# Linear attention with squared-ReLU feed-forward, FP32, one core: the first strip attended by pairs of heads, its queries loaded by POOL

## The chip, the cores and the metric

The kernel runs on one core of a Trainium2 chip. A core has five engines with an instruction queue each: PE (TensorE, matrix products and transposes), DVE (VectorE), ACT (ScalarE), POOL (GpSimd) and SP (SyncE, which here only issues DMAs). Each queue runs in order; the engines meet through semaphores. All DMAs, from whatever queue, run on the core's 16 DMA engines. The metric is the time of one execution on the device in microseconds; less is better.

## The reference

Everything is FP32, except that the two weight matrices arrive as 64-bit floats.

```
q, k, v: (8 batches, 8 heads, 576 tokens, 64);  g_norm: (64)
kv  = einsum('bhsd,bhse->bhde', k, v)               # 64 x 64 for each head
o   = einsum('bhsd,bhde->bhse', q, kv)
o   = o / sqrt(mean(o*o, last axis) + 1e-6) * g_norm
x   = o.transpose(0, 2, 1, 3).reshape(4608, 512)
h   = x @ w_in                                      # w_in: (512, 2048)
out = maximum(h, 0)**2 @ w_out                      # w_out: (2048, 512)
```

There is no softmax: queries meet a 64 x 64 state for each head. The key-value product of a head must be finished, over all tokens, before any of its queries can use it.

## The kernel before

**Tiling.** A token tile has 128 tokens (n), a strip has NT = 4 tiles, and there are 9 strips (s). A batch b has C = 4 whole tiles and a rest of 64 tokens; the rests of two batches form one tile. Heads go by pairs p, NP = 4 for a batch, so that a pair fills 128 partitions. Strip 0 is the four whole tiles of batch 0.

**Attention, in steps.** `transposed_query(b, p)` transposes a pair's queries on PE (L312) and copies them out on ACT (L314). `key_value(b, p)` forms k'v of the pair (L330), with the 64 rest tokens as its last two products, and copies the two blocks into a block diagonal on ACT (L332, L333). `query(n)` multiplies a tile's queries by the block diagonals of all four pairs (L362), squares on ACT (L371), sums on DVE (L372), and finds 1/sqrt with a root on ACT and a Newton step on DVE (`inverse_rms`), then scales (L388). `features(n)` transposes the result on PE (L414) and writes it with g_norm into xT (L415), the form that the feed-forward reads. For strip 0 `first_queries` does this for the four tiles together, after all four pairs: all products, then squares and sums tile by tile, one small 1/sqrt chain over 128x32, then scaling and transposes tile by tile.

**Feed-forward.** Strip 0 multiplies with w_in directly (`up_first`: 16 steps of four products, 128x512, L553). Then `down` multiplies with w_out by a scheme of seven products for a 2x2 block product (Strassen-Winograd), named 1 to 7, in two halves i each. Later strips use seven products on both sides. The order is ORDER = (1, 2, 6, 5, 7, 3, 4). Products share PSUM banks by BANK: 1, 6, 7 and 4 in A (of which there are two), 5 and 3 in B, 2 in C. Products 1, 5 and 2 open a bank; the others add into it. `combine` takes what is needed out between them: after 1, 6 and 5 ACT copies the bank into a snapshot (L529), after 2, 7 and 3 DVE adds bank and snapshot into the output.

**Weights.** The weights come as 64-bit floats in 32 pieces (`load_piece`, 512 KB each, eight buffers `raw`): 16 of w_in, 16 of w_out. A piece takes two operations on ACT (`convert_on_act`: L189, L192) and four on DVE (`convert_pieces`: L204, L207, L213, L218). The four buffers `w_c` between them bound how far ACT runs ahead. Pieces are converted two at a time; ACT is two pieces ahead of DVE. `up_first` of group g needs pieces 4g to 4g + 3. For w_out, `sums_out` also forms four sums and stores them; from these stores and those of L662 the blocks w_blk are streamed back (L597). `sums_in` forms the sums of w_in that later strips need, in the places of the first three w_out blocks.

**Order.** Nothing reorders the program: every engine runs its instructions as the Python code emits them. The attention steps stand in the list `slices`, in the order b, p; `attend(n)` emits the list up to n. Before strip 0 the steps of batch 0 are emitted with conversions between them as EARLY says, two conversions (pieces 0 to 3) in all, and ACT's operations for pieces 4 and 5. Then the steps of batch 1 are spread over the strip's up and down steps.

**Queues.** k and v go by SP, so do the pieces. The queries of pairs 0 to 2 of batch 0 go by ACT's queue, that of pair 3 by POOL's, later ones by SP. The rests of batch 0 (k_rest, v_rest, L129) go by ACT. The buffers of q, k and v are three deep: the fourth pair's loads wait until the first pair is used up.

Of the kernel before, what the change touches and what calls it, by code (L numbers as in the profile page):

```python
# [10 lines left out]
I32 = mybir.dt.int32  # L11
# [8 lines left out]
def kernel(  # L20
# [44 lines left out]
    STRIP = NT * P  # L65
    TH = STRIP // 2
    N_STRIP = N_TILE // NT
    EARLY = (0, 0, 0, 1, 1, 1, 1, 2)
    SQ = 32
    Q_ON_PE = 2  # L70
    X_ON_PE = 2
# [21 lines left out]

    def load(b, p, q_eng):
        hs = slice(2 * p, 2 * p + 2)
        for n, src, eng in (("k", k, nc.sync), ("v", v, nc.sync), ("q", q, q_eng)):
            whole = src[b, hs, 0 : C * P].rearrange("h (sp c) d -> sp h c d", c=C)
            if n == "q" and b >= Q_ON_PE:

                t = qkv_pool.tile([P, 4 * C, SQ], FP32, name=n, tag=n)  # L100
                for a in range(4):
                    h, f = divmod(a * SQ, D)
                    eng.dma_start(
                        out=t[ts(a, SQ)],
                        in_=src[b, 2 * p + h, 0 : C * P, f : f + SQ].rearrange("(i k) f -> i k f", k=4 * C),
                    )
            elif n != "q":
                t = qkv_pool.tile([P, 2, C, D], FP32, name=n, tag=n)
                eng.dma_start(out=t, in_=whole)
            else:  # L110

                t = qkv_pool.tile([P, C, 2, D], FP32, name=n, tag=n)
                for h in range(2):
                    eng.dma_start(out=t[:, :, h, :], in_=whole[:, h])
            main[n, b, p] = t
# [9 lines left out]
    def load_rest(b, eng):  # L125
        h = b % 2
        half = slice(REST * h, REST * (h + 1))
        for t, src in ((k_rest[half], k), (v_rest[half, h], v)):
            eng.dma_start(out=t, in_=src[b, :, C * P : S].rearrange("h s d -> s h d"))  # L129
# [20 lines left out]
    def load_next(q_eng=nc.sync):  # L150
        u = next(to_load, None)
        if u is not None:
            load(*u, q_eng)
# [20 lines left out]
    def load_piece():  # L174
        if len(raw) < len(sources):
            t = raw_pool.tile([P, 2, WN // 2], I64, name="raw", tag="raw")
            nc.sync.dma_start(out=t, in_=sources[len(raw)])
            raw.append(t)
# [6 lines left out]
    def convert_on_act(i):  # L185
# [6 lines left out]
        nc.scalar.activation(r, low, AF.Copy, scale=2.0**-29)  # L192
        words[i] = c, r, high

    def convert_pieces(ids, dests):

        for i in range(acted[0], min(ids[-1] + 3, len(sources))):
            convert_on_act(i)
            acted[0] = i + 1
        now = [words.pop(i) for i in ids]  # L200


        for c, _, _ in now:
            nc.vector.tensor_scalar(out=c, in0=c, scalar1=LEAST, scalar2=MOST, op0=ALU.max, op1=ALU.min)  # L204

        for c, _, _ in now:
            nc.vector.tensor_scalar(  # L207
                out=c.bitcast(I32), in0=c.bitcast(I32), scalar1=3, scalar2=0x3FFFFFFF,
                op0=ALU.logical_shift_left, op1=ALU.bitwise_and,
            )  # L210

        for c, _, high in now:
            nc.vector.scalar_tensor_tensor(  # L213
                out=c.bitcast(I32), in0=high, scalar=-(2**30), in1=c.bitcast(I32),
                op0=ALU.bitwise_and, op1=ALU.bitwise_or,
            )
        for (c, r, _), dest in zip(now, dests):
            nc.vector.tensor_tensor(out=dest.bitcast(I32), in0=c.bitcast(I32), in1=r, op=ALU.add)  # L218

        end = ids[-1] + 1  # L220
        while len(raw) < min(end + 8, max(len(sources) - 4, end + 4), len(sources)):
            load_piece()

# [32 lines left out]

    conversions = [(pieces_in, i) for i in range(0, NG * NP, 2)]
    conversions += [(pieces_out, j) for j in range(0, FQ, 2)] + [(sums_out, j) for j in range(0, FQ, 2)]
    converted = [0]

    def convert(n):
        while converted[0] < min(n, len(conversions)):
# [12 lines left out]
    one = const.tile([P, 1], FP32, name="one")  # L275
    nc.vector.memset(one, 1.0)
    nc.scalar.sqrt(one, one)
    load_next(nc.scalar)
    load_rest(0, nc.scalar)
    load_piece()  # L280
    load_piece()
    load_next(nc.scalar)
    load_next(nc.scalar)
    g_col = const.tile([P, 1], FP32, name="g_col")
    g_src = g_norm.rearrange("(d u) -> d u", u=1)
    for h in range(2):
# [36 lines left out]
    def key_value(b, p):  # L323
        tk, tv = main.pop(("k", b, p)), main.pop(("v", b, p))

        ps = apsum.tile([P, D], FP32, name="kv_ps", tag="at")
        for c in range(C + 1):
            for h in range(2):
                a, w = (tk[:, h, c, :], tv[:, h, c, :]) if c < C else (k_rest[:, 2 * p + h], v_rest[:, b % 2, 2 * p + h])
                nc.tensor.matmul(ps[ts(h, D)], lhsT=a, rhs=w, start=c == 0, stop=c == C)  # L330
        d = kv_all[:, (NP * b + p) % (2 * NP + 1)]
        nc.scalar.copy(d[0:D, 0:D], ps[0:D])  # L332
        nc.scalar.copy(d[D:P, D:P], ps[D:P])  # L333
        kvd[b, p] = d
        if b < 2:
            if p == 0:
                load_next(nc.sync if b else nc.gpsimd)
                if b == 0:
                    for _ in range(6):
                        load_piece()  # L340
        else:
            load_next()
            if p == NP - 1 and b + 1 < B:
                load_rest(b + 1, nc.sync)
                load_q_rest(b + 1, nc.sync)
# [16 lines left out]
                nc.tensor.matmul(o, lhsT=qT[b, p][:, c_b, :], rhs=kvd[b, p], start=True, stop=True)  # L362
        return ps

    def inverse_rms(tiles):

        n = len(tiles) * H
        ms = small.tile([P, NT * H], FP32, name="ms", tag="ms")[:, :n]
        for i, ps in enumerate(tiles):
            sq = xn_pool.tile([P, d_model], FP32, name="sq", tag="sq", bufs=1)  # L370
            nc.scalar.activation(sq, ps, AF.Square)  # L371
            nc.vector.reduce_sum(out=ms[:, ts(i, H)], in_=by_head(sq), axis=AX.X)  # L372
        nc.vector.tensor_scalar(out=ms, in0=ms, scalar1=1.0 / D, scalar2=EPS, op0=ALU.mult, op1=ALU.add)
        r = small.tile([P, NT * H], FP32, name="rms", tag="rms")[:, :n]
        nc.scalar.activation(r, ms, AF.Sqrt)
        nc.vector.reciprocal(r, r)

        t = small.tile([P, NT * H], FP32, name="newton", tag="newton")[:, :n]
        nc.vector.scalar_tensor_tensor(out=t, in0=ms, scalar=-0.5, in1=r, op0=ALU.mult, op1=ALU.mult)
        nc.vector.tensor_tensor(out=t, in0=t, in1=r, op=ALU.mult)  # L380
        nc.vector.scalar_tensor_tensor(out=r, in0=t, scalar=1.5, in1=r, op0=ALU.add, op1=ALU.mult)
        return r
# [8 lines left out]

    def query(n):
        ps = products_x(n)
        normalized(n, ps, inverse_rms([ps]))

    def first_queries():

        tiles = [products_x(n) for n in range(NT)]
        r = inverse_rms(tiles)
        for n, ps in enumerate(tiles):  # L400
            normalized(n, ps, r[:, ts(n, H)])
            features(n)

    def open_xt(s):
        if s not in xt:
# [50 lines left out]
    slices, ready = [], {}  # L456
    for b in range(B):
        for p in range(NP):
            slices += [(transposed_query, (b, p)), (key_value, (b, p))]
        first = b // 2 * PAIR + (C if b % 2 else 0)  # L460
        ns = list(range(first, first + C + b % 2))
        if b == 0:
            slices.append((first_queries, ()))
            ready[0] = len(slices)
            continue

        for i in range(len(ns) + 2):
            if i < len(ns):
                slices.append((query, (ns[i],)))
            if 0 < i <= len(ns):  # L470
                slices.append((features if b < X_ON_PE else squares_x, (ns[i - 1],)))
            done = ns[i - 1] if b < X_ON_PE and 0 < i <= len(ns) else ns[i - 2] if b >= X_ON_PE and i > 1 else None
            if done is not None:
                if b >= X_ON_PE:
                    slices.append((scale_x, (done,)))
                if done % NT == NT - 1:
                    if done // NT:
                        slices.append((sums_x, (done // NT,)))
                    ready[done // NT] = len(slices)
# [146 lines left out]

        combine(p, store(0, 0), store(0, 1), store(1, 0), store(1, 1))

    for i in range(ready[0] - 1):
        attend(i + 1)  # L630
        convert(EARLY[i])
    attend(ready[0])
    for s in range(N_STRIP):
        attend(ready[s])
        if s == 0:
# [1 line left out]
        else:  # L637
            steps = [(1, up, (s, g, p)) for g in range(NG) for p in ORDER]
        n_up = len(steps)
        steps += [(2, down, (s, p, i)) for p in ORDER for i in range(2)]  # L640
        goal = ready.get(s + 1, len(slices))
        total, done = sum(w for w, _, _ in steps), 0
        for i, (w, fn, a) in enumerate(steps):
# [23 lines left out]
                continue  # L667
            if i == n_up:
                sums_g(quarters(0, NG - 1))
            if i in (n_up + 6, n_up + 7):  # L670
                load_next()
            if i == n_up + 8:
                load_next()
                load_rest(2, nc.sync)
                load_q_rest(2, nc.sync)
                for g in range(NG):
                    sums_in(g)
# [36 lines left out]
```

## Time and profile before

| | us |
|---|---|
| three runs | 990.3, 993.07, 992.8; median 992.8 |
| the profiled execution | 993.63 |
| its span | 991.5 |
| PE busy, its share of the span | 956.9, 97% |
| DVE busy | 454.9, 46% |
| ACT busy | 244.5, 25% |
| PE busy in the first 45 us, from the stretches of 5 us | 17.3 |
| start of the first up product (L553) | 44.47 |
| start of the first down product (L519) | 107.80 |

Busy times are sums over instructions that may overlap. The span runs from the first to the last instruction; the execution's own time is 2.1 us longer. PE is busy without a gap worth naming after the first up product. So in the first 45 us the question is what PE waits for, and after it what PE has to do, or what would make it wait.

### The profile page before, as it was taken

What the parts mean: (1) busy time and instruction counts of PE and PEld (TensorE: products, weight loads), DVE (VectorE), ACT (ScalarE), POOL (GpSimd) and SP (SyncE); (2) the same over time, 40 slices, a digit from 0 to 9 for tenths busy, and PEclk for the clock granted to TensorE, in tenths of its full rate; (3) what the DMA queues carried; (4) which work ended last, traced back from release to release, by engine and by line L of the source; (5) the groups of instructions that cost most, each with busy time, mean ns of one, the idle gap of its engine ahead of it and who ended that gap; (6) DMA issues with size and microseconds to landing.
All of it is one profiled execution on the core that took longest, in us unless ns stands there. A gap on an engine that the chain in (4) does not pass through costs nothing.

```text
span 991.5 us, 12851 instructions
## 1 busy us (share of the span) xinstructions
PE 956.9 (97%) x4968; PEld 811.4 (82%) x4968; DVE 454.9 (46%) x811; ACT 244.5 (25%) x507; POOL 3.3 (0%) x9
## 2 busy tenths in 40 slices
PE   2599999999999999999999999999999999999997
PEld 2444788888888888888888888888888888888886
DVE  2799882464146523462346334442544255214420
ACT  2698411221022202211222113211321022002200
POOL 1000000000000000000000000000000000000000
PEclk9699999999999999999999999999999999999999
DMA  8599686325733462455333641466114610450041
GB/s 219 198 284 325 239 265 183 94 62 181 218 79 83 149 218 81 93 152 191 129 91 106 193 166 57 109 174 222 43 32 149 202 53 22 160 182 20 1 147 65
DMA packets 149148, 139.79 MB, mean 141 GB/s; under 512 B 83104, under 2 KB 129696, under 8 KB 141408
## 3 DMA queue, kind: packets, MB, share of 16 engines
q1 hardware_dynamic: 144608, 137.67, 45.3%
q10 hardware_dynamic: 4384, 1.05, 0.6%
q8 instruction: 39, 0.64, 0.3%
q0 software_dynamic: 96, 0.26, 0.1%
q14 instruction: 21, 0.17, 0.1%
HBM read 115.08 MB, written 23.86 MB: 140 GB/s over the span
## 4 chain that ended last, share of the span: by engine, by line
PE 96%; DMA 2%; DVE 1%; ACT 1%; issue 0%; SPq 0%; ACTq 0%; DVEq 0%
PE ps_A L519 48%; PE ps_B L519 24%; PE ps_C L519 12%; PE ps_A L553 3%; PE x_ps L362 3%; PE kv_ps L330 2%; PE ps_B L553 1%; PE ps_C L553 1%; DMA q<-in_q_dram 1%; DMA raw<-in_moe_w_in_dram 1%; PE xt_ps L414 1%; PE x_ps L357 0%; PE t_ps L312 0%; DVE ms L372 0%; ACT sq L371 0%
## 5 line engine op out<-in xcount | busy, mean ns | idle before, releaser
L519 PE MATMUL ps_A<-w_blk,gt 128*128 128x256 f32 x1120 | 249.1, 379 | 0.0
L519 PEld LDWEIGHTS ps_A<-w_blk,gt 128*128 128x128 f32 x1120 | 211.7, 190 | 28.5 <-issue 0.2
L519 PE MATMUL ps_A<-x_t,w_in 128*128 128x256 f32 x768 | 182.6, 381 | 0.7 <-DVE gt L578 0.7
L519 PEld LDWEIGHTS ps_A<-x_t,w_in 128*128 128x128 f32 x768 | 144.8, 190 | 20.9 <-DVE gt L578 1.1
L519 PE MATMUL ps_B<-w_blk,gt 128*128 128x256 f32 x544 | 121.0, 379 | 0.0
L519 PEld LDWEIGHTS ps_B<-w_blk,gt 128*128 128x128 f32 x544 | 103.0, 190 | 13.8
L529 ACT COPY snap<-ps_A 128x512 f32<-128x512 f32 x82 | 47.8, 584 | 184.4 <-PE ps_A L519 184.4
L225 DVE TENSOR_TENSOR gt<-gt 128x512 f32<-128x512 f32 (+1 forms) x54 | 66.2, 1226 | 42.0 <-PE ps_A L519 23.3
L578 DVE TENSOR_TENSOR gt<-ps_C,snap 128x512 f32<-128x512 f32 x32 | 22.1, 691 | 128.7 <-PE ps_C L519 128.7
L578 DVE TENSOR_TENSOR gt<-ps_A,snap 128x512 f32<-128x512 f32 x32 | 22.1, 691 | 102.2 <-PE ps_A L519 102.0
L579 DVE SCALAR_TENSOR_TENSOR gt<-gt 128x512 f32<-128x512 f32 x96 | 66.4, 692 | 3.3
L519 PE MATMUL ps_B<-xT,w_in 128*128 128x256 f32 x256 | 61.0, 381 | 0.0
L519 PE MATMUL ps_A<-xT,w_in 128*128 128x256 f32 x256 | 61.0, 381 | 0.0
L519 PE MATMUL ps_C<-xT,w_in 128*128 128x256 f32 x256 | 60.6, 379 | 0.0
L519 PE MATMUL ps_B<-x_t,w_in 128*128 128x256 f32 x256 | 60.5, 379 | 0.0
L372 DVE TENSOR_REDUCE ms<-sq 128x8 f32<-128x512 f32 x36 | 24.7, 685 | 77.8 <-ACT sq L371 77.8
L519 PE MATMUL ps_C<-w_blk,gt 128*128 128x256 f32 x256 | 57.5, 380 | 0.0
L519 PEld LDWEIGHTS ps_C<-xT,w_in 128*128 128x128 f32 x256 | 48.6, 190 | 6.7 <-issue 0.2
L519 PEld LDWEIGHTS ps_A<-xT,w_in 128*128 128x128 f32 x256 | 48.2, 190 | 6.7
L519 PEld LDWEIGHTS ps_B<-xT,w_in 128*128 128x128 f32 x256 | 48.2, 190 | 6.6
L519 PEld LDWEIGHTS ps_B<-x_t,w_in 128*128 128x128 f32 x256 | 48.3, 190 | 6.4
L519 PEld LDWEIGHTS ps_C<-w_blk,gt 128*128 128x128 f32 x256 | 48.2, 190 | 6.6 <-issue 0.2
(85 smaller groups left out, 767.2 us busy)
## 6 DMA issues: line engine op xcount, KB each, us to landing
w_blk<-w_out SPq DMA_DIRECT2D x60, 1024.0 KB, 5.2
k<-in_k_dram SPq DMA_DIRECT2D x32, 256.0 KB, 2.9
v<-in_v_dram SPq DMA_DIRECT2D x32, 256.0 KB, 3.2
raw<-in_moe_w_in_dram SPq DMA_DIRECT2D x16, 512.0 KB, 6.7
raw<-in_moe_w_out_dram SPq DMA_DIRECT2D x16, 512.0 KB, 5.2
x_d<-x_q SPq DMA_DIRECT2D x27, 256.0 KB, 2.4
xT<-x_d SPq DMA_DIRECT2D x108, 64.0 KB, 2.0
q<-in_q_dram SPq DMA_DIRECT2D x96, 64.0 KB, 3.2
```

What stands on the lines that cost most here:

```text
L225: eng.tensor_tensor(out=out, in0=a, in1=b, op=ALU.subtract)
L330: nc.tensor.matmul(ps[ts(h, D)], lhsT=a, rhs=w, start=c == 0, stop=c == C)
L362: nc.tensor.matmul(o, lhsT=qT[b, p][:, c_b, :], rhs=kvd[b, p], start=True, stop=True)
L372: nc.vector.reduce_sum(out=ms[:, ts(i, H)], in_=by_head(sq), axis=AX.X)
L414: nc.tensor.transpose(ps[:, p, :], t[:, ts(p, P)], ident)
L519: nc.tensor.matmul(bank[BANK[p]][:, i, :], lhsT=lhsT(k), rhs=rhs(k), start=p in (1, 5, 2) and i == 0 and k == 0, stop=k == n - 1, skip_gro ...
L529: nc.scalar.copy(snap[p], b)
L553: nc.tensor.matmul(ps, lhsT=w_in[:, kc % KH, g, kc // KH * 2 + fh, ts(i, P)], rhs=xt[0][:, :, kc, :], start=kc == 0, stop=kc == NP - 1,)
L578: nc.vector.tensor_tensor(out=o, in0=b, in1=a, op=ALU.add)
L579: nc.vector.scalar_tensor_tensor(out=o, in0=o, scalar=0.0, in1=o, op0=ALU.max, op1=ALU.mult)
```

## The change

1. The attention of strip 0 goes by pairs of heads instead of by tiles. `first_queries(p)` multiplies the four tiles' queries of one pair, in one PSUM tile; `first_normalized(p)` scales them; `first_features(p)` transposes them into xT. The last two of pair p stand after the key-value product of pair p + 1. Since the mean goes over one head's 64 columns, a pair has all that it needs. The 1/sqrt chain runs four times, over 128x8.
2. One w_in piece is converted with each pair: ACT's two operations before the pair's transposes, the first two of DVE ahead of the sum of squares, the third before the 1/sqrt, the fourth after the scaling. ACT's operations for pieces 4 and 5 stand before the last pair's 1/sqrt. EARLY goes.
3. The loads: for each pair a piece, then k and v on SP, and all four queries on POOL. The last of these queries has the buffer of q_rest, so that four are in flight. The rests stay on ACT.
4. In strip 0 the down products go 1, 2, 5, 6, 7, 3, 4, with 6 and 5 in exchanged places, and the loads of batch 2 and the sums of w_in come two half products earlier.

The inverse root is written as two functions, `mean_squares` and `inverse_root`; for later tiles they emit what `inverse_rms` did.

```diff
-    EARLY = (0, 0, 0, 1, 1, 1, 1, 2)
...
     def load(b, p, q_eng):
         hs = slice(2 * p, 2 * p + 2)
+        first_rest = (b, p) == (0, NP - 1)
...
-                t = qkv_pool.tile([P, C, 2, D], FP32, name=n, tag=n)
+                pool, tag = (rest_pool, "q_rest") if first_rest else (qkv_pool, n)
+                t = pool.tile([P, C, 2, D], FP32, name=n, tag=tag)
...
+    def conversion(i, dest):
+        c, r, high = words.pop(i)
+        ci = c.bitcast(I32)
+        yield nc.vector.tensor_scalar(out=c, in0=c, scalar1=LEAST, scalar2=MOST, op0=ALU.max, op1=ALU.min)
+        yield nc.vector.tensor_scalar(
+            out=ci, in0=ci, scalar1=3, scalar2=0x3FFFFFFF, op0=ALU.logical_shift_left, op1=ALU.bitwise_and
+        )
+        yield nc.vector.scalar_tensor_tensor(
+            out=ci, in0=high, scalar=-(2**30), in1=ci, op0=ALU.bitwise_and, op1=ALU.bitwise_or
+        )
+        yield nc.vector.tensor_tensor(out=dest.bitcast(I32), in0=ci, in1=r, op=ALU.add)
...
-    converted = [0]
+    converted = [NP // 2]
...
-    load_next(nc.scalar)
-    load_rest(0, nc.scalar)
-    load_piece()
-    load_piece()
-    load_next(nc.scalar)
-    load_next(nc.scalar)
+    for p in range(NP):
+        load_piece()
+        load_next(nc.gpsimd)
+        if p == 0:
+            load_rest(0, nc.scalar)
+    load_more(0)
...
         if b < 2:
-            if p == 0:
-                load_next(nc.sync if b else nc.gpsimd)
-                if b == 0:
-                    for _ in range(6):
-                        load_piece()
+            if b == 1 and p == 0:
+                load_next()
...
-    def first_queries():
-        tiles = [products_x(n) for n in range(NT)]
-        r = inverse_rms(tiles)
-        for n, ps in enumerate(tiles):
-            normalized(n, ps, r[:, ts(n, H)])
-            features(n)
+    def first_queries(p):
+        ps = apsum.tile([P, NT, P], FP32, name="x_ps", tag="at")
+        for n in range(NT):
+            nc.tensor.matmul(ps[:, n, :], lhsT=qT[0, p][:, n, :], rhs=kvd[0, p], start=True, stop=True)
+        steps = conversion(p, w_in[:, p % KH, 0, p // KH * 2 : p // KH * 2 + 2])
+        next(steps)
+        next(steps)
+        first[p] = flat(ps), mean_squares(flat(ps)), steps
+
+    def first_normalized(p):
+        ps, ms, steps = first.pop(p)
+        next(steps)
+        x_n["first", p] = t = xn_pool.tile([P, NT, P], FP32, name="x_n", tag="x_n")
+        r = inverse_root(ms)
+        nc.vector.tensor_tensor(
+            out=by_head(flat(t)), in0=by_head(ps), in1=r.unsqueeze(2).to_broadcast([P, H, D]), op=ALU.mult
+        )
+        for _ in steps:
+            pass
+
+    def first_features(p):
+        t, x = x_n.pop(("first", p)), open_xt(0)
+        ps = apsum.tile([P, NT, P], FP32, name="xt_ps", tag="at")
+        for n in range(NT):
+            nc.tensor.transpose(ps[:, n, :], t[:, n, :], ident)
+        nc.scalar.activation(x[:, :, p, :], flat(ps).rearrange("p (a t) -> p a t", t=SQ), AF.Copy, scale=g_col)
...
         for p in range(NP):
-            slices += [(transposed_query, (b, p)), (key_value, (b, p))]
+            if b:
+                slices += [(transposed_query, (b, p)), (key_value, (b, p))]
+                continue
+            slices += [(convert_on_act, (p,)), (transposed_query, (b, p)), (key_value, (b, p))]
+            if p > 0:
+                slices.append((first_normalized, (p - 1,)))
+            slices.append((first_queries, (p,)))
+            if p > 0:
+                slices.append((first_features, (p - 1,)))
...
-            slices.append((first_queries, ()))
+            slices += [(first_normalized, (NP - 1,)), (first_features, (NP - 1,))]
...
-    for i in range(ready[0] - 1):
-        attend(i + 1)
-        convert(EARLY[i])
-    attend(ready[0])
+    attend(ready[0] - 2)
+    for i in range(NP, NP + 2):
+        convert_on_act(i)
+    acted[0] = NP + 2
...
-        steps += [(2, down, (s, p, i)) for p in ORDER for i in range(2)]
+        steps += [(2, down, (s, p, i)) for p in (ORDER if s else (1, 2, 5, 6, 7, 3, 4)) for i in range(2)]
...
-            if i in (n_up + 6, n_up + 7):
+            if i in (n_up + 4, n_up + 5):
                 load_next()
-            if i == n_up + 8:
+            if i == n_up + 6:
                 load_next()
                 load_rest(2, nc.sync)
                 load_q_rest(2, nc.sync)
```

`load_more(end)` is the loop at the end of `convert_pieces`, now a function of its own: it loads pieces until eight beyond `end` are under way.

More of the change, by code (lines that the diff above doesn't have):

```diff
@@ L199, in convert_pieces, with load_more @@
             acted[0] = i + 1
[L200 to L220, printed above, removed]
+        for _ in zip(*[conversion(i, dest) for i, dest in zip(ids, dests)]):
+            pass
+        load_more(ids[-1] + 1)
+    def load_more(end):
         while len(raw) < min(end + 8, max(len(sources) - 4, end + 4), len(sources)):
@@ L363, in products_x, with mean_squares, inverse_root @@
         return ps
[L365 to L372, printed above, removed]
+    def mean_squares(ps):
+        n = ps.shape[-1] // D
+        sq = xn_pool.tile([P, d_model], FP32, name="sq", tag="sq", bufs=1)
+        nc.scalar.activation(sq, ps, AF.Square)
+        ms = small.tile([P, H], FP32, name="ms", tag="ms")
+        nc.vector.reduce_sum(out=ms, in_=by_head(sq), axis=AX.X)
         nc.vector.tensor_scalar(out=ms, in0=ms, scalar1=1.0 / D, scalar2=EPS, op0=ALU.mult, op1=ALU.add)
-        r = small.tile([P, NT * H], FP32, name="rms", tag="rms")[:, :n]
+        return ms
+    def inverse_root(ms):
+        r = small.tile([P, H], FP32, name="rms", tag="rms")
         nc.scalar.activation(r, ms, AF.Sqrt)
         nc.vector.reciprocal(r, r)
-        t = small.tile([P, NT * H], FP32, name="newton", tag="newton")[:, :n]
+        t = small.tile([P, H], FP32, name="newton", tag="newton")
         nc.vector.scalar_tensor_tensor(out=t, in0=ms, scalar=-0.5, in1=r, op0=ALU.mult, op1=ALU.mult)
@@ L393, in query @@
         ps = products_x(n)
-        normalized(n, ps, inverse_rms([ps]))
-    def first_queries():
-        tiles = [products_x(n) for n in range(NT)]
-        r = inverse_rms(tiles)
-        for n, ps in enumerate(tiles):
-            normalized(n, ps, r[:, ts(n, H)])
-            features(n)
+        normalized(n, ps, inverse_root(mean_squares(ps)))
+    first = {}
+    def first_queries(p):
[15 more added lines that the diff above has]
+        for _ in steps:
+            pass
+    def first_features(p):
[4 more added lines that the diff above has]
+        nc.scalar.activation(x[:, :, p, :], flat(ps).rearrange("p (a t) -> p a t", t=SQ), AF.Copy, scale=g_col)
     def open_xt(s):
@@ L458 @@
         for p in range(NP):
-            slices += [(transposed_query, (b, p)), (key_value, (b, p))]
-        first = b // 2 * PAIR + (C if b % 2 else 0)
-        ns = list(range(first, first + C + b % 2))
+            if b:
[7 more added lines that the diff above has]
+                slices.append((first_features, (p - 1,)))
+        first_n = b // 2 * PAIR + (C if b % 2 else 0)
+        ns = list(range(first_n, first_n + C + b % 2))
         if b == 0:
-            slices.append((first_queries, ()))
+            slices += [(first_normalized, (NP - 1,)), (first_features, (NP - 1,))]
             ready[0] = len(slices)
```

## The prediction

> **What bounds the kernel now.** I read the page's chain by engine first, then the chain in order of time over the first 50 us, the timeline around 44, 113 and 135 us, and the DMA queues and issues.
>
> ```profile
> PE 96%; DMA 2%; DVE 1%; ACT 1%; issue 0%; SPq 0%; ACTq 0%; DVEq 0%
> 2.54 9.32 DMA q<-in_q_dram
> 11.88 2.84 DMA q<-in_q_dram
> 15.85 1.29 PE kv_ps L330 x20
> 18.75 7.51 DMA raw<-in_moe_w_in_dram
> 26.28 0.66 ACT w_c L189
> 28.26 4.92 PE x_ps L362 x24
> 38.95 0.70 DVE x_n L388
> 39.79 1.94 PE xt_ps L414 x8
> 44.47 5.75 PE ps_A L553 x7
> ```
>
> PE is the chain from 44.47 us, where the first up product starts, to the end of the 991.5 us. What is not PE lies ahead of it: queries land (14.7), pieces 2 and 3 land (26.26) and are converted on ACT ahead of the copies of pairs 2 and 3, then sixteen products, four squares and four reductions in turn, and one normalization. So the change is worth what it moves 44.47, less what it opens later.
>
> ```profile
> 42.38 0.76 DVE L204 TENSOR_SCALAR w_c<-w_c 128x512 f32<-128x512 f32 x2
> 113.24 0.69 DVE L372 TENSOR_REDUCE ms<-sq 128x8 f32<-128x512 f32 x1 [1.37 <-ACT sq L371]
> 116.92 0.60 PE L414 MATMUL xt_ps<-ident,x_n 128*128 128x128 f32 x4
> 134.93 0.58 ACT L529 COPY snap<-ps_A 128x512 f32<-128x512 f32 x1 [1.63 <-PE ps_A L519]
> 135.16 7.07 PE L519 MATMUL ps_B<-w_in,gt 128*128 128x256 f32 x32
> ```
>
> DVE converts without a pause from 42.38 to 111.9, beside the up products, and then has 1.37 us to spare before the first query of batch 1. PE transposes that query at 116.92, 0.9 us after it is normalized (116.01). At 134.93 ACT copies bank A away while PE already works in bank B.
>
> ```profile
> q10 hardware_dynamic: 4384, 1.05, 0.6%
> q0 software_dynamic: 96, 0.26, 0.1%
> k_rest<-in_k_dram ACTq DMA_DIRECT2D x1, 128.0 KB, 11.1
> v_rest<-in_v_dram ACTq DMA_DIRECT2D x1, 128.0 KB, 8.2
> ```
>
> ACT's queue (q10) moves packets of 240 bytes, POOL's (q0) of 2.7 KB on average. The two rests land at about 15.2 and 15.6 us (issue 4.05 and 7.36 plus these), and the first key-value product ends only after them.
>
> **What the Trainium skill says.** "DMA: Bandwidth & Descriptors", section Queues, rings and completion order: each DMA engine takes turns between its queues packet by packet; section SWDGE vs HWDGE vs iDMA: a software packet gathers up to 64 descriptors and 4096 B. The packet sizes above agree. So queries on POOL's queue get a large share per turn, and the rests on ACT's, in small packets, a small one. "TensorE: Matmul & The Clock Gate", Part 1: after an idle window of about 3.4 us PE runs at half clock until a window was busy. The trace agrees: the granted clock is 0.50 from 39.9 to 50.1 us, and eight product instructions take 1.64 us there or in 28 to 33 (24 in 4.92), against 1.05 at 116.03.
>
> **The change, part by part.**
>
> *Loads.* ACT loses six query issues (two at 2.54, four from 11.88 to 16.58), so its first copy no longer waits until 17.95. POOL gets eight, 0.81 each in the rows of before, after its memset: 2.3 to 8.8 us. On SP each piece goes before its pair's keys and values. In the compiled order the third v waits for k_rest to land, and the fourth k for v_rest and for the first key-value product; SP holds raw 3 to 7 behind these. The pair chain starts when the rests land, R. Before, 3.0 MB had moved by then, from 2.2 us: 225 GB/s. Now 2 MB of SP, 1 MB of queries and 0.25 MB of rests lie ahead or beside: 3.25 MB, at 225 to 250 GB/s 13.0 to 14.4 us, so R is 15.2 to 16.7; I take 16.1. Bounds: 12.3, if the rests take only the 8.2 us of v_rest from 4.05; 20.0, if raw 2 and the third k are in front too (4.0 MB). Nothing else stands on POOL. Everything else is in by R + 8: behind R come v of pair 2, raw 3, k and v of pair 3, raw 4 and 5, 2.0 MB at the 380 GB/s of 28 to 32 us, 5.3 us and some 2 to land; the first use of raw 4 is at R + 18, of pair 3 at R + 13. If that cover went, ACT's last root would stand behind the conversions of raw 4 and 5, us for us. The last pair's q takes the q_rest buffer, whose next load comes long after.
>
> *Pairs.* Per pair, PE: transposes, key-value, products, transposes of the pair before; 3.3 us at full clock, 5.0 at half. From R to the pair's copies: 0.8 (half clock 0.95). To those of pair 1: 0.14 to PE, products 1.05, square 0.07 + 0.60, two conversions 1.13, copies 0.48 + 0.43: 3.9 (4.7 at half clock). Then a ring through three engines sets the pace: root to normalized 0.03 + 1.84 (114.17 to 116.01 in the trace), 0.13, transposes 0.60, 0.10, ACT scale 0.69, conversion 1.04, copies 0.48 + 0.40: 5.3 (5.9), twice. DVE has 4.4 us of work in it and is hidden.
> *Tail.* After the last copies: the ring to the scale of pair 2, 3.4; pieces 4 and 5 on ACT, ahead of the last root, 2.2, of which 0.9 is more than the reduction beside them needs; root to normalized 1.84, transposes 0.73: 8.15 (8.9).
> Sum: R + 23.5 at full clock, R + 26.4 at half; PE will be between, R + 24.9 = 41.0 for the first up product. That is -3.45 us. The three further small chains (0.88 us of DVE each) are inside these figures. The sixteen conversions on DVE are the same instructions, split.
>
> *DVE later.* Its long run starts after the last normalization and one add (0.6), at about the first up product, where before it had started 2.1 us ahead. The spare 1.37 and 0.9 us hold 2.27, so 0 to 1 us is lost; I take 0.3. The half clock at the first up products cost 2.8 us before (5.6 us at half) and I expect the same; were it less, DVE would be the limit and take it back.
>
> *Order of the first down products, 1 2 5 6 7.* Product 7 adds into the bank of 6 directly after it, and must wait for the copy of 6 (0.07 + 0.58 + 0.14): +0.8 us, once; before, product 5 stood between. Product 5 earlier costs nothing: its sums are done some 13 us ahead. The loads of batch 2 and the sums of w_in move up by one product; product 5 has read its block by then. Nothing on PE waits for them within 20 us. On DVE the add of product 7 stands behind the sums, and these wait for the end of product 5 and the three block stores (L662, the last issued by 125.3); if the stores came 5 us late, product 3 (6.9 us) would still cover it, which stands between 7 and product 4 on the same bank.
>
> Total: -3.45 + 0.8 + 0.3 = -2.35 us. The profiled execution took 993.63 (span 991.5 and 2.1 around it), 0.08% over the median 992.8. So 991.3 against it, 990.5 on the median.
>
> **Rivals.**
> *Early rests:* R about 12.8 and PE at full clock: first up product at 36.3, -8.2 + 0.8 + 0.3: 985.7, or 987.5 with a part at half clock. For it: ACT's queue holds half the small packets it held. Against: before, its first packets moved only near 6.5 us, and POOL's big ones come now.
> *Rests starved (slower):* ACT's queue gives way to POOL's and SP's packets, R is 21, PE stays at half clock: 47.4, +2.9 + 1.1: 996.8. At half clock it decides from R = 17.0 (no gain) and is over 0.3% from 20.0. For it: 240 against 2,700 bytes a turn, and SP's own loads wait behind the rests. Against: POOL's queries are done after 1 MB.
> *DVE becomes the limit:* queries of batch 1 stall PE by some 2 us more, because conversions start with the up products; 992.5. For it: DVE is full from 42 to 112. Against: it starts only 2 us later relative to PE.
>
> **How the numbers follow.** Forecast 0.45 (own range 988.5 to 992.5), early rests 0.27, starved 0.20, DVE 0.08. A measurement of this kernel tells 0.3%, 3 us, from no change (990.3 to 993.1 in three runs). Faster by more (under 989.8): 0.27 and some 0.13 of the forecast, 0.40. Slower (over 995.8): 0.18, nearly all of the starved case. Same: 0.42. The range reaches into both sides: 985.8 to 995.5.
>
> **What would show it.** The first L585 product at 39 to 43 us; rests landing at 15 to 17; 5.3 to 5.9 us from one pair's copies to the next; two conversions between the last square and the last root; one idle of 0.8 us of PE ahead of product 7; DVE without a pause to about 68 us after the first up product. I am wrong if the rests land outside 14 to 18, if a pair takes over 7 us, or if PE waits for DVE or DMA between 45 and 140 us.

## The result, and the profile after

| | before | after |
|---|---|---|
| median of the runs, us | 992.5 (990.3 to 993.07, 4 runs) | 993.2 (992.84 to 993.48, 4 runs) |
| ratio after / before | | 1.0011, 95% interval 0.9994 to 1.0028 |
| span of the profiled execution, us | 991.5 | 991.6 |
| first up product | 44.47 | 43.33 |
| first down product | 107.80 | 105.32 |
| last output copy on ACT begins | 985.34 | 984.83 |

No change that can be told from none. The forecast (990.5) was 2.7 us too low: the measured median lies 0.7 above the forecast's own range (988.5 to 992.5) and inside the wide one (985.8 to 995.5). The lower part of the table shows two single executions: a gain of 1.14 us at the first up product, 2.48 at the first down product, 0.51 at the end of the arithmetic, and nothing in the span, because the last stores took 0.6 us longer in this execution. The profiled execution before took 993.63 us, 1.1 over its median; the one after took 993.41, 0.2 over its own. So these gains are some 0.9 us larger than the medians would have them.

First the page of the changed kernel, its chain by engine and two of its DMA queues (packets, MB, share):

```profile
PE 90%; DVE 4%; DMA 3%; ACT 1%; issue 1%; ACTq 0%; DVEq 0%
...
q0 software_dynamic: 384, 1.05, 0.4%
...
q10 hardware_dynamic: 1216, 0.26, 0.2%
```

PE carried 96% of the chain before and carries 90% now. DVE and DMA have taken its place, although PE is still busy for nearly the whole span. The queues show that the queries did move: POOL's q0 carries 1.05 MB in packets of 2.7 KB, ACT's q10 little but the two rests.

Now the timeline of the changed kernel, in order of time (start, duration, instruction; in brackets the engine's idle time before it and what ended it):

```profile
10.60 1.09 PE L315 MATMUL t_ps<-ident,q 128*128 128x128 f32 x4 [10.60 <-DMA q<-in_q_dram]
11.62 1.12 PE L333 MATMUL kv_ps<-v,k 128*64 128x64 f32 x16
18.27 0.48 PE L333 MATMUL kv_ps<-v_rest,k_rest 128*64 128x64 f32 x4 [5.53 <-DMA v_rest<-in_v_dram]
...
19.07 0.21 ACT L336 COPY kv_all<-kv_ps 64x64 f32<-64x64 f32 x1
...
23.85 0.21 ACT L336 COPY kv_all<-kv_ps 64x64 f32<-64x64 f32 x1
...
29.59 0.21 ACT L336 COPY kv_all<-kv_ps 64x64 f32<-64x64 f32 x1
...
34.87 0.21 ACT L336 COPY kv_all<-kv_ps 64x64 f32<-64x64 f32 x1
...
43.33 4.85 PE L585 MATMUL ps_A<-xT,w_in 128*128 128x512 f32 x8
...
115.21 0.66 PE L437 MATMUL xt_ps<-ident,x_n 128*128 128x128 f32 x4 [0.60 <-DVE x_n L389]
...
124.99 3.62 PE L551 MATMUL ps_B<-w_in,gt 128*128 128x256 f32 x16
...
141.41 7.17 PE L551 MATMUL ps_A<-w_blk,gt 128*128 128x256 f32 x32 [0.68 <-ACT snap L561]
```

The first pair's queries land at 10.6, 4 us earlier than before, and its keys and values are multiplied by 12.7. Then PE stands still for 5.5 us until the values of the rest tokens land. From there the pairs follow one another at 4.8, 5.7 and 5.3 us (the L336 copies), and 8.5 us lie between the start of the last of these copies and the first up product. The two later waits of PE are new. The timeline of the kernel before, at its third and fifth down product, shows no wait (and none ahead of the query's transposes at 116.92):

```profile
126.48 3.62 PE L519 MATMUL ps_A<-w_blk,gt 128*128 128x256 f32 x16
...
142.07 7.07 PE L519 MATMUL ps_A<-w_blk,gt 128*128 128x256 f32 x32
```

### The profile page after: what moved, and what is told of

It reads as the page before. It is cut to its first block, busy times and chain, and to the rows that moved or that the text cites. A ratio compares the mean times of both kernels' runs of the same rounds, so it can differ in the third digit from the quotient of the medians.

```text
span 991.6 us, 12873 instructions
## 1 busy us (share of the span) xinstructions
PE 956.9 (97%) x4968; PEld 811.1 (82%) x4968; DVE 457.0 (46%) x826; ACT 244.8 (25%) x510; POOL 7.7 (1%) x15
## 3 DMA queue, kind: packets, MB, share of 16 engines
q0 software_dynamic: 384, 1.05, 0.4%
## 4 chain that ended last, share of the span: by engine, by line
PE 90%; DVE 4%; DMA 3%; ACT 1%; issue 1%; ACTq 0%; DVEq 0%
PE ps_A L551 47%; PE ps_B L551 24%; PE ps_C L551 12%; PE x_ps L362 2%; PE kv_ps L333 2%; DMA v_rest<-in_v_dram 1%; PE ps_A L585 1%; DVE wt L228 1%; DMA raw<-in_moe_w_out_dram 1%; PE ps_B L585 1%; DVE w_c L208 1%; DMA k_rest<-in_k_dram 1%; PE x_ps L403 0%; ACT w_c L190 0%; PE ps_C L585 0%
```

## The experiments

Times are medians, and ratios are to the kernel before, measured beside each group on the same chip: 992.55 us (25 runs) for the first four experiments, 992.47 (35 runs) for the next four, 992.18 (17 runs) for the last. The changed kernel itself was not measured again: "against the changed kernel" means against its 993.2 us of four runs.

**1. The rests on POOL's queue.** The first suspect is the late landing of the rests.

```diff
-            load_rest(0, nc.scalar)
+            load_rest(0, nc.gpsimd)
```

> The changed kernel with the two rests of batch 0 issued on POOL's queue, right after the first pair's queries, instead of on ACT's. Theory 'rests': in the changed kernel everything ahead of the up products hangs on the rests, which land at 18.1 us because ACT's small packets take turns with larger ones; on POOL they land at about 9 to 10, the first key-value product then ends with its other products at about 12.7 (18.75 now), and the first up product moves 6 us, from 43.3 to about 37.3: 987.2 us. Rival 'bytes': the same 5 MB must come in, so pieces 2 and 3 or k and v of pair 3 hold the later pairs; first up product not before 41.5, 991.5 us or more. Rival 'DVE': the up products move by 6 us, but the queries of batch 1 wait longer than the 0.6 us they wait now; 989 to 991.

Measured: 988.4 us (988.25 to 989.15), ratio 0.9953 (0.994 to 0.9967). The timeline of this kernel:

```profile
12.66 0.48 PE L333 MATMUL kv_ps<-v_rest,k_rest 128*64 128x64 f32 x4
...
13.46 0.21 ACT L336 COPY kv_all<-kv_ps 64x64 f32<-64x64 f32 x1
...
38.18 5.61 PE L585 MATMUL ps_A<-xT,w_in 128*128 128x512 f32 x8
```

The wait ahead of the rest products is gone. The copies come 5.6 us earlier, the first up product 5.15, and the time falls by 4.8 against the changed kernel; the theory had 37.3 us for the first up product and 987.2 for the time, so about 1 us of its gain is missing. On POOL's queue the rests are also no small packets any more: q0 carries 480 packets and 1.31 MB here, against 384 and 1.05 in the changed kernel, so the 0.26 MB of the rests went in 96 packets of 2.7 KB. The landing of the rests, and not the pace of the pairs, was thus what held the start.

**2. The old order of the down products, with the loads of batch 2 and the sums of w_in back in their old places.**

```diff
-for p in (ORDER if s else (1, 2, 5, 6, 7, 3, 4))
+for p in ORDER
...
-            if i in (n_up + 4, n_up + 5):
+            if i in (n_up + 6, n_up + 7):
...
-            if i == n_up + 6:
+            if i == n_up + 8:
```

> The changed kernel with the first strip's down products in the old order 1 2 6 5 7 3 4, and the loads and sums beside them two half products later again. Theory: the idle 0.68 us of PE ahead of product 7, which waits for the copy of bank A after 6, goes: -0.8 us against the changed kernel, 992.4. Rival: the streamed block of product 6 is not there when PE comes to it, about 125 us, and PE waits there instead: the same or slower.

Measured: 992.65 us, ratio 0.9999 (0.9991 to 1.0007). That is 0.55 below the changed kernel, which is less than these medians tell apart. The timeline shows the mechanism all the same: between products 6 and 7 stands product 5 again, and nothing waits.

```profile
129.66 3.62 PE L551 MATMUL ps_A<-w_blk,gt 128*128 128x256 f32 x16
133.11 0.60 PE L437 MATMUL xt_ps<-ident,x_n 128*128 128x128 f32 x4
133.55 7.07 PE L551 MATMUL ps_B<-w_in,gt 128*128 128x256 f32 x32
140.46 7.07 PE L551 MATMUL ps_A<-w_blk,gt 128*128 128x256 f32 x32
```

**3. ACT's operations for pieces 4 and 5 behind the last root instead of ahead of it.**

```diff
-    for i in range(NP, NP + 2):
-        convert_on_act(i)
     acted[0] = NP + 2
...
         r = inverse_root(ms)
+        if p == NP - 1:
+            for i in range(NP, NP + 2):
+                convert_on_act(i)
```

> The changed kernel with ACT's two operations each for pieces 4 and 5 after the last pair's root instead of before it. Theory: they hold the root from 39.2 to 40.5 us; the first up product comes at 42.0 instead of 43.3, -1.3 us: 991.9. Rival: they only move the wait, to DVE, which then finds pieces 4 and 5 not ready, or to the last scale on ACT: within 0.3 us of the changed kernel, 993.

Measured: 992.41 us, ratio 0.9998 (0.999 to 1.0006), 0.8 below the changed kernel, again at the edge of what can be told. The timeline of this kernel:

```profile
35.42 0.21 ACT L336 COPY kv_all<-kv_ps 64x64 f32<-64x64 f32 x1
...
39.72 0.21 ACT L376 ACTIVATE rms<-ms 128x8 f32<-128x8 f32 x1 [0.73 <-DVE ms L371]
39.84 0.65 ACT L190 ACTIVATE w_c<-raw 128x512 f32<-128x512 f32 x1
...
42.34 0.97 PE L588 MATMUL ps_A<-xT,w_in 128*128 128x512 f32 x1
```

The root now waits for DVE's sum alone and comes 0.8 us earlier (40.53 in the changed kernel); the first up product comes 1.0 us earlier. The edit itself is worth more: the last pair's copy came 0.55 us later here (35.42 against 34.87), so counted from that copy the root is 1.4 us earlier and the first up product 1.5.

**4. The three together.** The diff is the sum of the three above.

> The three edits together: rests on POOL, old order of the down products, pieces 4 and 5 after the last root. If they add: -6 - 0.8 - 1.3 against the changed kernel, 985.1 us, first up product at about 36. Rival 'DVE': from 100 us on PE waits for DVE (the queries of batch 1, or the block of product 6), and it is 987 or more.

Measured: 985.65 us (985.03 to 986.33), ratio 0.9924 (0.9911 to 0.9936). This beats both kernels. From its timeline, the first pair's copy, the first up product and the first query of batch 1:

```profile
13.79 0.21 ACT L336 COPY kv_all<-kv_ps 64x64 f32<-64x64 f32 x1
...
36.53 5.29 PE L588 MATMUL ps_A<-xT,w_in 128*128 128x512 f32 x8
...
108.41 0.66 PE L440 MATMUL xt_ps<-ident,x_n 128*128 128x128 f32 x4 [0.15 <-DVE x_n L389]
```

Against the changed kernel the first copies move by 5.28 us, the first up product by 6.80 and the query's transposes still by 6.80. With the 0.68 ahead of product 7 that makes 7.5, and the medians differ by 7.55. The theory had 985.1. The three edits one by one gave 4.8, 0.55 and 0.8, which is 1.4 less than together; the late copy in experiment 3 hides some 0.5 of this, and the rest was not traced.

**5. By tiles, rests on POOL.** Would the kernel before have gained from the same edit? The diff is that of experiment 1, in the kernel before.

> The kernel before (attention by tiles, queries 0 to 2 on ACT's queue), with the two rests of batch 0 issued by POOL. Theory: in the tile-wise order the rests are not what the first up product waits for (the landing of the queries at 14.7 and of pieces 2 and 3 at 26.3 us are), so the gain of moving the rests exists only with pairs: 992.5, within 991.3 to 993.0, first up product at 43.3 to 44.5 us. Rival: the rests cost the same in either order, or their packets hold up the queries too: 988.0 to 989.5, first up product near 40 us.

Measured: 992.46 us, ratio 0.9998 (0.9989 to 1.0006). Its first up product starts at 44.42, against 44.47. In the order by tiles the rests are not waited for, as the theory said: the same edit is worth 4.8 us with pairs and nothing with tiles.

**6. Experiment 4 with the queries of pairs 0 to 2 back on ACT's queue.**

```diff
-        load_next(nc.gpsimd)
+        load_next(nc.scalar if p < 3 else nc.gpsimd)
```

> Like e4_all (rests on POOL, old order of the down products, pieces 4 and 5 after the last root), with the queries of pairs 0 to 2 back on ACT's queue. Theory: small packets on ACT's queue get a small share beside SP's and POOL's, whatever they carry: the queries of pair 0 land at 13.5 to 15 us in place of 10.6, the copies of pair 0 come at 16.5 to 18 us in place of 13.6, and all moves by 3 to 4.5 us: 988.7 to 990.2 against 985.65. Rival: only the rests suffer on ACT's queue, queries land as early there: 985.2 to 986.5.

Measured: 991.52 us (990.63 to 992.42), ratio 0.999 (0.9984 to 0.9997). The theory had the direction, but expected 3 to 4.5 us of loss where it is 5.9. The timeline of this kernel:

```profile
15.67 1.09 PE L315 MATMUL t_ps<-ident,q 128*128 128x128 f32 x4 [15.67 <-DMA q<-in_q_dram]
...
19.55 0.21 ACT L336 COPY kv_all<-kv_ps 64x64 f32<-64x64 f32 x1
...
42.46 5.12 PE L588 MATMUL ps_A<-xT,w_in 128*128 128x512 f32 x8
```

The queries land at 15.67, 5 us later than on POOL's queue, and ACT comes free even later: its six query issues take 11.9 us (POOL took 6.05 for eight in the changed kernel), the two small loads behind them last until 17.7, and only then does ACT convert piece 0 and copy. The expectation counted the landing and forgot the engine that issues. So the copies come 5.8 us later than in experiment 4, and all of it reaches the time.

**7. Experiment 4 with the rests at the head of SP's queue.** Is it the queue, or the small size of these packets?

```diff
     for p in range(NP):
+        if p == 0:
+            load_rest(0, nc.sync)
         load_piece()
         load_next(nc.gpsimd)
-        if p == 0:
-            load_rest(0, nc.gpsimd)
```

> Like e4_all, with the two rests first on SP's queue, ahead of piece 0, in place of POOL's. Theory: what made the rests late was the share of ACT's queue, not the small size of their packets; at the head of SP's queue they land by 8 us, the rest of SP's loads comes about 1 us later, and the queries on POOL (10.6 us) stay what the first pair waits for: 985.0 to 987.0. Rival: packets of 256 bytes are slow on any hardware queue, so the rests take 8 us or more there too and hold up the pieces and keys behind them on SP: 989 or more.

Measured: 987.38 us (986.94 to 988.96), ratio 0.995 (0.9938 to 0.9962), just over the theory's upper end (987.0) and under the rival's 989. DMA issues of this kernel that begin in the first 12 us (KB each, median us from issue to landing):

```profile
v<-in_v_dram SPq DMA_DIRECT2D x3, 256.0 KB, 9.8
k_rest<-in_k_dram SPq DMA_DIRECT2D x1, 128.0 KB, 2.8
v_rest<-in_v_dram SPq DMA_DIRECT2D x1, 128.0 KB, 4.0
```

The same two loads that took 12.8 and 14.8 us on ACT's queue take 2.8 and 4.0 us here, in packets that are just as small (1,056 for 0.26 MB, by the totals of SP's queue). So these packets are not slow by themselves; what is beside and ahead of them decides. Queue and place changed together here, and no run puts the rests on SP's queue behind other loads. The price is paid by what stands behind. The timeline of the same kernel shows PE waiting for the first pair's v instead, and the copies are 1.34 us later than in experiment 4.

```profile
8.23 1.08 PE L315 MATMUL t_ps<-ident,q 128*128 128x128 f32 x4 [8.23 <-DMA q<-in_q_dram]
13.49 1.12 PE L333 MATMUL kv_ps<-v,k 128*64 128x64 f32 x16 [4.17 <-DMA v<-in_v_dram]
```

**8. DVE's load doubled in one place.** The clamp of pieces 4 to 11 is done twice, which changes no value.

```diff
         yield nc.vector.tensor_scalar(out=c, in0=c, scalar1=LEAST, scalar2=MOST, op0=ALU.max, op1=ALU.min)
+        if 4 <= i < 12:
+            nc.vector.tensor_scalar(out=c, in0=c, scalar1=LEAST, scalar2=MOST, op0=ALU.max, op1=ALU.min)
```

> The changed kernel, with the clamp of pieces 4 to 11 (L202) done twice: 8 x 0.417 us = 3.3 us more on DVE between the first up product and the first query of batch 1, and no other change. Theory: DVE sets the end of this stage, PE waits for it already (0.60 us), so all of it shows: 3.3 us more than 993.2, 996.5 (995.8 to 997.0), PE's wait ahead of that query's transposes 3.5 to 4.0 us. Rival: DVE has slack there or catches up behind it, and the wait of 0.60 us was a single meeting: at most 1 us more, 992.8 to 994.2.

Measured: 997.71 us (997.15 to 1000.69), ratio 1.0056 (1.0043 to 1.0069): 4.5 us over the changed kernel by the medians (the theory had 2.6 to 3.8), 3.8 by the spans (995.4 and 991.6). The timeline shows where the 3.3 us of DVE surfaced:

```profile
77.15 0.33 PE L323 MATMUL tr_ps<-ident,q_rest 128*128 128x128 f32 x1 [1.08 <-DMA q_rest<-in_q_dram]
...
111.83 0.43 PE L359 MATMUL x_ps<-kv_all,qT_rest 128*64 128x128 f32 x2 [0.47 <-ACT kv_all L338]
...
119.06 0.66 PE L439 MATMUL xt_ps<-ident,x_n 128*128 128x128 f32 x4 [2.25 <-DVE x_n L391]
```

1.08 + 0.47 + 2.25 = 3.80 us of waits, against 0.60 in the changed kernel: 3.2 us more. Only part of it came where it was expected: ahead of the query's transposes stand 2.25 us, not 3.5 to 4.0. The first wait is for a load that came late. Its issue on SP's queue came 4.0 us later than in the changed kernel (68.62 against 64.62), and from 44 us up to that issue the queue had waited 16.8 us for the last steps of w_in's conversions on DVE, against 13.1. So DVE does set the end of this stage, and in the changed kernel's execution there was no slack left in it.

**9. By tiles, with all queries and the rests on POOL.** How much of experiment 4 is the loads alone?

```diff
-    load_next(nc.scalar)
-    load_rest(0, nc.scalar)
+    load_next(nc.gpsimd)
+    load_rest(0, nc.gpsimd)
...
-    load_next(nc.scalar)
-    load_next(nc.scalar)
+    load_next(nc.gpsimd)
+    load_next(nc.gpsimd)
```

> The kernel before (attention by tiles), with the queries of all four pairs and the two rests of batch 0 on POOL's queue, nothing of them on ACT's. Theory: the loads alone give a good part of what e4_all gives, because in the tile-wise order the fourth pair's keys and pieces 2 and 3 are issued on SP only when pair 0 is used up, and pair 0 waits for its queries: with these at 10.6 us in place of 14.8 pieces 2 and 3 land near 22.5 us in place of 26.3, and the first up product comes 3.5 to 4.5 us earlier, near 40.3: 988.0 to 989.5. Rival: the pieces land no earlier, since what was loaded earlier only takes their place in the DMA engines, and the pair order is needed for any gain: 991.5 to 993.

Measured: 991.31 us (989.5 to 993.08), ratio 0.9993 (0.9985 to 1.0002), next to the rival's range and far from the theory's. The timeline of this kernel:

```profile
11.36 1.09 PE L312 MATMUL t_ps<-ident,q 128*128 128x128 f32 x4 [11.36 <-DMA q<-in_q_dram]
...
24.07 0.68 ACT L189 ACTIVATE w_c<-raw 128x512 f32<-128x512 f32 x1
...
42.29 3.70 PE L553 MATMUL ps_A<-xT,w_in 128*128 128x512 f32 x8 [0.78 <-ACT xT L415]
```

The queries land 3.4 us earlier than before. The last piece that the copies wait for is converted from 24.07 us (26.28 before), and the first up product comes 2.2 us earlier, so the theory was right in kind: the pieces do move up with the first pair, by 2.2 where it expected 3.8. The medians differ by only 0.9. This trace can't say where the rest goes, for it is of a short execution: 989.77 us, 1.5 under its median, with a first down product at 103.14, 4.7 us ahead of the kernel before.

Pairs and loads need each other. In medians against the kernel before, measured beside each: tiles with the rests on POOL 0.0; tiles with everything on POOL -0.9; pairs (with the mends of experiments 2 and 3) with the queries on ACT -0.95; pairs with everything on POOL -6.9.

## Why the prediction was near, and which step failed

**The rests, R.** This is the step that failed: "R is 15.2 to 16.7; I take 16.1". The rests landed at 18.1 (v_rest: issue at 3.30 and 14.8 us to landing), inside the bounds (12.3 to 20.0) but 2.0 us late, and just outside the 14 to 18 that the prediction gave as a sign of being wrong. The queues of the changed kernel up to then, from 0 to 18.2 us (packets, MB, share):

```profile
q1 hardware_dynamic: 2395, 3.11, 61.2%
q0 software_dynamic: 384, 1.05, 21.7%
q10 hardware_dynamic: 1216, 0.26, 8.8%
```

The term that was mis-sized is the bytes, "ahead or beside: 3.25 MB": 3.11 + 1.05 + 0.26 = 4.42 MB had moved. The prediction counted 2 MB of SP's loads; 3.1 MB went. Piece 2 had been issued at 5.59 and the third k at 10.41 us, and both shared the engines with the rests. The upper bound had named exactly these two loads. The rate was better than assumed: 4.42 MB in the 15.9 us from 2.2 to 18.1 are 278 GB/s, against 225 to 250. The two errors offset in part. The same queues of the changed kernel from 12 to 18.2 us:

```profile
q1 hardware_dynamic: 1069, 1.30, 75.1%
q10 hardware_dynamic: 845, 0.17, 17.0%
```

ACT's queue got four packets to SP's five, but 0.2 KB in each, where SP's had 1.2. That is what the Trainium skill states in "DMA: Bandwidth & Descriptors", section Queues, rings and completion order: the engines take turns packet by packet. The trace agrees, and shows the consequence that the prediction named and priced too low: where turns are equal, bytes are not. The turns are not the whole delay: ACT's queue moved its first packet only between 7 and 8 us. How much of the 18.1 us is this late start and how much the turns after it, no run separates.

**Pairs and tail.** Right in sum. 4.8, 5.7 and 5.3 us from copy to copy against 3.9 to 4.7, 5.3 to 5.9 twice; 8.25 us from the end of the last copy to the first up product against 8.15 to 8.9. From R 25.2 us, predicted 24.9. One term in it was too small: the price of pieces 4 and 5 ahead of the last root, "0.9", was 1.4. DVE had the last pair's sum ready at 39.14, the root started at 40.53; and experiment 3, counted from its last copy, gains 1.4 at the root.

**First up product.** 43.33 instead of 41.0: -1.14 where -3.45 was forecast. 2.0 of the 2.3 us are R.

**The clock.** "I expect the same" did not hold in this pair of executions. The up products took 61.99 us (43.33 to 105.32) against 63.33 before, 1.34 less. The stretch from 45 to 50 us (PE, weight loads, DVE, ACT, POOL busy, granted clock, DMA share, GB/s) in the kernel before:

```profile
45.00:50.00 5.00, 5.00 (x7) 1.88 (x6) 5.00 (x12) 4.54 (x9) 0.00 (x0) 0.55 0.56 161
```

In the kernel of experiment 5, whose PE work is the same and which begins its up products at the same time (44.42):

```profile
45.00:50.00 5.00, 5.00 (x10) 2.04 (x9) 5.00 (x11) 4.57 (x9) 0.00 (x0) 0.75 0.56 169
```

And in the changed kernel:

```profile
45.00:50.00 5.00, 5.00 (x12) 2.24 (x11) 5.00 (x11) 3.91 (x8) 0.00 (x0) 0.92 0.70 209
```

In stretches of half a microsecond the recorded clock is full from 49.5 us in the kernel before (the prediction had 50.1), from 47.5 in experiment 5 and from about 45.8 in the changed kernel. That is 5.0, 3.1 and 2.5 us after the first up product. The two executions by tiles thus differ by 2 us of half clock, and experiment 5's up products took 62.38 us, 0.95 less. Over all traces the up products took 60.85 to 63.33 us by tiles (three traces) and 61.99 to 63.32 by pairs (eight). So the 1.34 us lie within what comes and goes without the change, and are not to be credited to it.

**DVE.** The place was right, the size was not: "0 to 1 us is lost; I take 0.3". Between the first down product (-2.48) and the third product's start (124.99 against 126.48, -1.49) 0.99 us went: 0.77 between the first query's products and its transposes (1.66 us from start to start, against 0.89), where the profile books the wait of 0.60, and most of the rest at the second query. This wait for DVE is the other thing that the prediction named as a sign of being wrong. It also said that DVE would take back what a shorter half clock gives, and the other traces fit that in the main: experiments 2 and 7, also by pairs, whose up products took 63.00 and 63.32 us, show no wait for DVE, and took 18.69 us from the first down product to the third, as the kernel before (18.68; 19.67 in the changed kernel). It is not one for one: experiment 1 waits 0.79 us with up products of 62.75. Experiment 8 shows that DVE is the limit in the changed kernel's execution. The rival "DVE becomes the limit" was thus right in its place, but at most half its size (0.99 of 2 us), and not in every execution.

**Product 7.** Right: a wait of 0.68 us for the copy of bank A, and the lead fell by 0.84 us; predicted 0.8. It is gone in experiment 2.

**Sum.** -1.14 (first up product), -1.34 (clock), +0.99 (DVE), +0.84 (product 7) and about +0.1 unassigned give the -0.51 at the last output copy. The forecast was -2.35. The largest error, 2.0 us, is R. That the sum came as near to the forecast as it did owes something to luck: without the clock's share, which was no part of the change, the end would have been later; but DVE would then have taken back less, so these two don't simply subtract.

**The rivals.** "Early rests" did not happen in the changed kernel, but experiment 4 is nearly that case: 985.65 us, where the rival had 985.7, although by another sum, since there products 6 and 7 are apart again and pieces 4 and 5 moved. "Rests starved" was nearer than its chance of 0.20 suggests: R passed the 17.0 from which it would decide at half clock and stayed below 20; but PE was slow only for half of the pairs. The eight products of the first and of the last pair, in the changed kernel:

```profile
19.42 2.05 PE L403 MATMUL x_ps<-kv_all,qT 128*128 128x128 f32 x8 [0.67 <-ACT kv_all L336]
...
35.13 1.16 PE L403 MATMUL x_ps<-kv_all,qT 128*128 128x128 f32 x8 [1.52 <-ACT kv_all L336]
```

The number of "DVE becomes the limit", 992.5, is the nearest of all to the measured 993.2, but its own account, a start as early as forecast and then 2 us more of waiting for DVE, is not what happened.

The medians of before and after differ by 0.7 us and the spans by only 0.1, because the profiled execution before was a long one: 1.1 us over its median, with up products at the long end of all traces (63.33). Whether the changed kernel is really slower by 0.7 stays open (the interval of the ratio includes 1). So does where the rest of experiment 9's earlier start goes.

## What to carry to other kernels

A reordering that shortens a chain is worth only what its first input allows: before pricing the steps, list every load that is under way when the chain's first input lands, those for later steps too, and divide by the rate. Here the small packets on a queue of their own, beside queues with larger ones, landed last (18.1 us). Putting the few small loads that the start waits for on POOL's queue, in packets of 2.7 KB, or at the head of SP's queue mended it; then see what stands behind them. Where an engine has been full for tens of microseconds beside PE, as DVE is here, more work on it can come back as a wait at the end of its run (3.3 us of work as 3.2 us of waits in experiment 8).

## What the runs showed of the hardware

The same two loads of 128 KB took 12.8 and 14.8 us from issue to landing on ACT's queue, 8.4 and 8.3 on POOL's (experiment 4), and 2.8 and 4.0 at the head of SP's (experiment 7). ACT's queue moved its first packet between 7 and 8 us, some 4.5 us after the first issue at 2.54; in the kernel before between 6 and 7. Six query loads and two small ones issued by ACT kept that engine from computing until 17.7 us (experiment 6; the six alone took 11.9 us), while POOL issued eight query loads in 6.05 us in the changed kernel. And the moment at which PE's clock comes up differed by 2 us between two executions of the same PE work (before and experiment 5), which was worth 0.95 us of up products.
